# Value product of a decode attention block: weights stationary in four column groups instead of values stationary

## The chip, the cores and the metric

The kernel runs on one core of a Trainium2 chip. The metric is the device time of one execution in microseconds, as the median of several runs. They agree within 0.6% (kernel before), so differences under one per cent are read from ratios with an interval. A ratio is the mean time of one kernel's fast runs over the mean of the other's in the same rounds. It is therefore not quite the ratio of the medians that are quoted beside it.

## The reference, cut to what matters

The program is one decode step: four sequences, one new token each, 16 query heads in pairs over 8 key/value heads, a cache of 8192 positions and head size 256. A small MLP (cut here) gates the result.

```python
B, Sq, D = 4, 1, 448
Hq, Hkv, Sk, Dh = 16, 8, 8192, 256
q = (x @ wq)                                                  # x is layer-normalized
scores = einsum("bhqd,bhkd->bhqk", q, k) * Dh ** -0.5         # k, v repeated for 2 query heads
p = softmax(scores)
o = einsum("bhqk,bhkd->bhqd", p, v)                           # the value product
s = o.reshape(B, Sq, Hq * Dh) @ wo
out = x_in + s * silu(mlp(x))                                 # mlp cut
```

There are 4 x 8 = 32 pairs of sequence and key/value head. The text calls each of them a *head*. Each has 4 MB of K and 4 MB of V (bf16), which are read once: 268 MB of the 279 MB that the kernel loads.

## The kernel before

Per head, TensorE transposes K (128 transposes of 128x128), ScalarE and VectorE copy the transposes from PSUM, TensorE forms the scores (128 matmuls with the transposed K as stationary weights), and the value product of the head two places earlier is made with V as stationary weights. K and V have two buffers each. A new load is issued when TensorE has used up the buffer.

```python
def f_pv(h, lo, hi):                       # PE: value product of head h
    if lo == 0:
        take(pe, "v_ot"); take(pe, "dv%d" % (h % 2), 16)      # V has landed
    for i in range(lo, hi):                # 128 in all: two halves of Dh, 64 chunks of 128 positions
        dh, kk = divmod(i, NCH)
        ins = pe.matmul(psv[:, dh * PVW:(dh + 1) * PVW],      # out 128 x 32
                        vb[:, h % 2, kk, dh:DH:NHALF],        # stationary: V, 128 x 128
                        pT[:, h % 2, kk * REP:kk * REP + PVW],  # streaming: weights, 32 wide, 2 of use
                        start=(kk == 0), stop=(kk == NCH - 1))

def body(h):                               # PE, one head; the loop has two of them in one pass
    for j in range(NGR):                   # 16 groups of 8 transposes
        f_t(h, j)
        if j >= LAG: f_s(h, j - LAG)       # 8 score matmuls
        if j == J_SUM: f_sum(h - 1)
    tail = [the last three f_s] + [f_rmaxT(h), f_bc(h)]
    for i, f in enumerate(tail):
        f_pv(h - 2, PV_PARTS[i], PV_PARTS[i + 1]); f()

# SP queue: who releases a load
load_k(h): wait_ge(S["v_k"], h - 1)        # K of head h-2 transposed and copied
load_v(h): wait_ge(S["v_v"], h + 1)        # value product that last used the buffer is done
# ... (cut: projections, MLP, softmax pieces, the tail)
```

After the loop comes a *tail*: the value product of the last head but one, the output projection, and the last V, which arrives in four pieces.

Of the kernel before, what the change touches and what calls it, by code (L numbers as in the profile page):

```python
# [32 lines left out]
def bass_recurrent_scan__gqa_block_cached__mixer_s_mlp__decode_kernel(  # L33
# [40 lines left out]
    LAG = 3  # L74
    assert NGR == 16 and NGR % NST == 0 and NGR % RING == 0
    D_GROUPS = (0, 2, 4, 6, 8, 10, 12, 14, 15)
    NPV = NCH * NHALF
    PV_PARTS = (0, 12, 24, 44, 86, NPV)
    J_SUM = 3
    PVW = 32  # L80
    PIECES = (0, 32, 48, 56, NCH)
    NPIECE = len(PIECES) - 1
# [4 lines left out]
    with ExitStack() as es:  # L87
        def sb(name, shape, dty):
# [15 lines left out]
        xn2T = sb("xn2T", [P, DK, NHF, Bn], BF16)  # L104
        par = sb("par", [P, NHF], F32)
        hT = sb("hT", [P, NFK, NHF, Bn], BF16)
        rmax = sb("rmax", [P, REP], F32)
        negb = sb("negb", [P, 2, REP], F32)
        rowsum = sb("rowsum", [P, 2, REP], F32)
# [26 lines left out]
        S = {n: es.enter_context(nc.semaphore(n)) for n in (  # L136
            ["dx", "dwq", "dw3", "dw4", "dwo", "dk0", "dk1", "dv0", "dv1", "dout"]
            + ["dvl%d" % i for i in range(NPIECE)]
            + ["p_td", "p_ta", "p_sc", "p_m1", "p_m2", "p_m3", "p_pv", "p_x", "p_q", "p_h", "p_h2", "p_o"]
            + ["v_ev", "a_ev", "v_rmax", "v_diag", "v_neg", "v_ot", "a_exp", "g_q", "g_c",  # L140
               "v_s", "v_k", "v_v", "g_o", "g_p", "g_f", "v_xT", "v_qT", "v_hT", "v_bout", "v_c", "v_w", "a_c", "v_out"])}


        vflat = [vb[:, i].rearrange("p c d -> p (c d)") for i in range(2)]
# [73 lines left out]
        def prog_pool(gp):  # L218
            def put(h):
                b, g = divmod(h, HKV)  # L220
                gp.tensor_copy(OT[:, g, :, :, b],
                               otmp[:, h % 2].rearrange("p dh r -> p r dh")
                               ).then_inc(S["g_p"], 1)
                gp.wait_ge(S["g_p"], h + 1)
                gp.sem_inc(S["g_o"], 1)

            c = _Chain(gp, S["g_c"])
            c(gp.memset(ident_f[:, :], 0.0))
            c(gp.memset(ident_b[:, :], 0.0))
            c(gp.memset(ones_f[:, :], 1.0))  # L230
            c(gp.memset(pT[:, :, :].rearrange("p s n -> p (s n)"), 0.0))
            c(gp.memset(vflat[1][:, DK * HDH:NCH * DH], 0.0))
            c(gp.memset(vflat[0][:, DK * FH + NF * D:NCH * DH], 0.0))
            c(gp.memset(rowsum[:, :, :].rearrange("p s r -> p (s r)"), 1.0))
            c(gp.memset(rz[:, :, :].rearrange("p s r -> p (s r)"), 1.0))
            c.sync()
            for t in (ident_b, ident_f):
                c(gp.affine_select(out=t[:, :], in_=t[:, :], compare_op=ALU.not_equal, fill=1.0,  # L238
                                   base=0, pattern=[[-1, P]], channel_multiplier=1))
            gp.wait_ge(S["v_qT"], 1)  # L240
            for h in range(NH):
                b, g = divmod(h, HKV)
                if h >= 2:
                    gp.wait_ge(S["v_v"], h - 1)
                gp.tensor_copy(qc[:, h % 2], qT[:, b, g]).then_inc(S["g_q"], 1)  # L245
                if h >= 4:
                    put(h - 4)
            for h in range(NH, NH + 2):
                gp.wait_ge(S["v_v"], h - 1)
                put(h - 4)  # L250
            gp.wait_ge(S["g_p"], NH - 2)
            gp.sem_inc(S["g_f"], 1)

        def evac(engine, h, j):
# [8 lines left out]
        def prog_act(act):  # L263
            act.dma_start(x_sb[:, :], x2d).then_inc(S["dx"], 16)
            c = _Chain(act, S["a_c"])
            for k, col in ((1, 0), (2, 8)):
                act.wait_ge(S["v_w"], k)
                c(act.activation(st[:, col + 2:col + 3], st[:, col + 1:col + 2], ACT.Sqrt))
            act.wait_ge(S["v_w"], 3)
            c(act.activation(gel_b[:, :], gel_a[:, :], ACT.Tanh))  # L270
            act.wait_ge(S["v_w"], 4)
            c(act.activation(sg[:, :], bout[:, :], ACT.Tanh, scale=0.5))

            def exps(h):
                s = h % 2
                take(act, "v_neg")
                sc = psc[s][:, 0:NCH * REP].rearrange("p (k h) -> p k h", h=REP)
                pv_p = pT[:, s, 0:NCH * REP].rearrange("p (k h) -> p k h", h=REP)
                for hh in range(REP):
                    ins = act.activation(pv_p[:, :, hh], sc[:, :, hh], ACT.Exp,  # L280
                                         bias=negb[:, s, hh:hh + 1], scale=SCALE,
                                         accum_out=rowsum[:, s, hh:hh + 1])
                    if hh == REP - 1:
                        ins.then_inc(S["a_exp"], 1)

            with nc.Fori(0, NH // 2, engines=[mybir.EngineType.Activation]):
                for h in range(2):
                    for j in range(NGR):
                        if j not in D_GROUPS:
                            evac(act, h, j)  # L290
                    exps(h)
            act.wait_ge(S["v_out"], 1)
            store(act, 2)
            store(act, 3)

        def prog_dve(v):
# [31 lines left out]



            v.sem_inc(S["v_ot"], 1)
            v.sem_inc(S["g_o"], 4)
            v.sem_inc(S["a_exp"], 1)
            v.sem_inc(S["dv0"], 16)
            v.sem_inc(S["dv1"], 16)
            c(v.memset(h2_ps[:, 0:DQ], 0.0))
# [6 lines left out]
            xn_mark = c.n  # L343
            layernorm(xn_f, xn2_f, xn2_b, 8, 2)
            xn2_mark = c.n
            v.wait_ge(S["g_c"], 10)
            idv = ident_f[:, :].rearrange("p (m t) -> p t m", t=NHF)
            c(v.tensor_reduce(par[:, :], idv, AX.X, ALU.add))
            c.sync()
            for k, dst in ((0, xnT), (1, xn2T)):  # L350
                v.wait_ge(S["p_x"], k + 1)
# [62 lines left out]
                             ).then_inc(S["v_s"], 1)  # L414
                take(v, "v_s")

            def f_ot(h):
                take(v, "p_pv")
                take(v, "g_o")
                v.tensor_tensor(otmp[:, h % 2],  # L420
                                psv[:, 0:NHALF * PVW].rearrange("p (a n) -> p a n", a=NHALF)[
                                    :, :, 0:REP],
                                rz[:, h % 2, :].unsqueeze(1).broadcast_to([P, NHALF, REP]),
                                ALU.mult).then_inc(S["v_s"], 1)
                take(v, "v_s")
                v.sem_inc(S["v_ot"], 1)
                v.sem_inc(S["v_v"], 1)  # L427

            with nc.Fori(0, NH // 2, engines=[mybir.EngineType.DVE]):
                for h in range(2):  # L430
                    for j in range(NGR):
                        if j in D_GROUPS:
                            evac(v, h, j)
                        if j == J_SUM + 1:
                            f_rz(h - 1)
                    v.sem_inc(S["v_k"], 1)
                    f_rmax(h)
                    f_diag(h)
                    f_ot(h - 2)
                    f_negb(h)  # L440
            f_rz(NH - 1)
            for h in (NH - 2, NH - 1):
                b, g = divmod(h, HKV)
                take(v, "p_pv")
                for dh in range(NHALF):
                    src = psc[0] if (h == NH - 1 and dh == 1) else psv
                    ins = v.tensor_tensor(OT[:, g, :, dh, b],
                                          src[:, dh * PVW:dh * PVW + REP],
                                          rz[:, h % 2, :], ALU.mult)
                ins.then_inc(S["v_ot"], 1)  # L450
            v.wait_ge(S["p_o"], 1)
            c(v.tensor_tensor(res[:, :], o_ps[:, 0:DQ], sg[:, :], ALU.mult))  # L452
            c.sync()
# [1 line left out]
            return xn_mark, xn2_mark  # L455

        def prog_pe(pe, xn_mark, xn2_mark):
            pe.wait_ge(S["g_c"], 10)
            for k, (src, mark) in enumerate(((xn_b, xn_mark), (xn2_b, xn2_mark))):
                pe.wait_ge(S["v_c"], mark)  # L460
                for j in range(DK):
# [74 lines left out]
            def f_pv(h, lo, hi):  # L536
                if lo == 0:
                    take(pe, "v_ot")
                    take(pe, "dv%d" % (h % 2), 16)
                for i in range(lo, hi):  # L540
                    dh, kk = divmod(i, NCH)
                    ins = pe.matmul(psv[:, dh * PVW:(dh + 1) * PVW],  # L542
                                    vb[:, h % 2, kk, dh:DH:NHALF],
                                    pT[:, h % 2, kk * REP:kk * REP + PVW], start=(kk == 0), stop=(kk == NCH - 1))
                if hi == NPV:
                    ins.then_inc(S["p_pv"], 1)

            def body(h):
                for j in range(NGR):
                    f_t(h, j)  # L550
                    if j >= LAG:
                        f_s(h, j - LAG)
                    if j == J_SUM:
                        f_sum(h - 1)
                tail = [lambda j=j: f_s(h, j) for j in range(NGR - LAG, NGR)]
                tail += [lambda: f_rmaxT(h), lambda: f_bc(h)]
                for i, f in enumerate(tail):
                    f_pv(h - 2, PV_PARTS[i], PV_PARTS[i + 1])
                    f()
# [9 lines left out]
            def f_o(g):  # L569
# [6 lines left out]
                                        start=(k == 0), stop=(k == NKC - 1))  # L576
                return ins

            f_sum(h)
            pe.wait_ge(S["g_f"], 1)  # L580
            for g in range(HKV - 2):
                f_o(g)
            f_pv(h - 1, 0, NPV)
            take(pe, "v_ot")
            f_o(HKV - 2)
            for i in range(NPIECE):
                take(pe, "dvl%d" % i, 16)
                for dh in range(NHALF):
                    for kk in range(PIECES[i], PIECES[i + 1]):
                        ins = pe.matmul((psv, psc[0])[dh][:, dh * PVW:(dh + 1) * PVW],  # L590
                                        kn[:, 1 - h % 2, kk, dh:DH:NHALF],
                                        pT[:, h % 2, kk * REP:kk * REP + PVW], start=(kk == 0),
                                        stop=(kk == NCH - 1))
# [54 lines left out]
```

## Time and profile before

| | before |
|---|---|
| time, median of 4 runs | 664.05 us (662.49 to 665.04) |
| span of the profiled run | 660.5 us |
| loads | 279 MB, queue busy 98.8% of the span |
| TensorE busy | 81% |
| load rate between 334 and 640 us | 432 GB/s |

The first lines are from the page of the kernel before: the busy time of the engines, the DMA packets, the load queue's share, the groups of the transposes and the value product (line, engine, operation, operands, count, busy us, mean ns, idle time just before them and what ended it), and the K loads (count, size, median us from issue to landing).

```profile
PE 535.4 (81%) x13065; PEld 530.5 (80%) x13065; DVE 252.3 (38%) x548; ACT 254.9 (39%) x358; POOL 17.0 (3%) x76
...
DMA packets 12325, 279.20 MB, mean 423 GB/s; under 512 B 1172, under 2 KB 3224, under 8 KB 3736
...
q1 hardware_dynamic: 12288, 278.99, 98.8%
...
L504 PE MATMUL pst<-ident_b,kn 128*128 128x128 bf16 x4096 | 347.0, 241 | 92.7 <-PEq L216 92.6
...
L542 PE MATMUL psv<-pT,vb 128*128 128x32 bf16 x4224 | 130.3, 177 | 7.8 <-issue 7.7
L542 PEld LDWEIGHTS psv<-pT,vb 128*128 128x128 bf16 x4224 | 119.2, 97 | 8.8 <-issue 8.2
...
kn<-in_A_k_cache_dram SPq DMA_DIRECT2D x32, 4096.0 KB, 26.6
```

TensorE is busy for 81% of the span and the load queue for 98.8%. The waits view of the same kernel, between 330 and 640 us, tells what ended TensorE's idle time (total us, times, longest):

```profile
PE pst L504 <- PEq L216: 50.5, 16, 3.8
```

These 16 waits of 3.2 us on average are all before the first transposes of a head, that is, for its K. The windows view of 334 to 640 us has the load rate in its last column, the share of the DMA engines and TensorE's granted clock before it:

```profile
334.00:640.00 306.00, 258.25 (x6170) 256.75 (x6169) 117.06 (x236) 125.25 (x172) 4.59 (x29) 0.85 1.00 432
```

The timeline of the kernel before around the end of one head (start us, us, engine, what; in brackets the idle time before):

```profile
307.05 0.33 SPq L180 DMA_DIRECT2D kn<-in_A_k_cache_dram  x1
...
308.57 1.21 PE L542 MATMUL psv<-pT,vb 128*128 128x32 bf16 x42
...
309.63 0.27 PE L524 MATMUL psm<-ident_f,rmax 128*2 128x128 f32 x1
...
309.74 1.21 PE L542 MATMUL psv<-pT,vb 128*128 128x32 bf16 x42
...
311.64 0.33 SPq L188 DMA_DIRECT2D vb<-in_A_v_cache_dram  x1
...
314.40 3.57 PE L504 MATMUL pst<-ident_b,kn 128*128 128x128 bf16 x32 [3.15 <-PEq L216]
```

Here 42 value matmuls take 1.21 us. After the value product TensorE idles 3.15 us for the next K, which was asked for long before. A K load lands 26.6 us after its issue by the page's DMA part, though 4 MB take only 9.7 us at this rate. So loads queue up behind each other, and between 334 and 640 us the queue never runs dry (DMA share 1.00).

### The profile page before, as it was taken

Reading aid. Unit: us, or ns where it says so; the run is one execution under the profiler, and the core shown is the slowest. Engines: PE = TensorE matmul, PEld = TensorE weight load, DVE = VectorE, ACT = ScalarE, POOL = GpSimd, SP = SyncE. Lnnn points to the kernel's source line nnn. Section 1 sums busy time; section 2 is a strip of 40 time slices with the busy share of each in tenths; the row PEclk is TensorE's granted clock in tenths of the full one; section 3 lists DMA queues with packets and bytes.
Section 4 is the critical chain, followed back from the end, with each engine's and each line's share of the span. In section 5 each row is a group of like instructions: output and inputs, shape, how many; then the busy total and the mean of one; then the engine's idle time right before and its main releaser. Section 6 shows DMA issues by size and latency. Waiting matters only on the chain. (4 is left out here: it accounts for less than half of the span.)

```text
span 660.5 us, 29043 instructions
## 1 busy us (share of the span) xinstructions
PE 535.4 (81%) x13065; PEld 530.5 (80%) x13065; DVE 252.3 (38%) x548; ACT 254.9 (39%) x358; POOL 17.0 (3%) x76
## 2 busy tenths in 40 slices
PE   1487799967789878878987887898878898887886
PEld 1487799967789878878987787898878898887785
DVE  6233255433334433334443333433333343333340
ACT  1044355433344443334443343444333444433340
POOL 4000000000000000000000000000000000000000
PEclk9997799977898877889887788987878997787896
DMA  8999999999999999999999999999999999999995
GB/s 363 440 402 434 415 419 427 439 417 433 425 443 429 429 437 423 443 429 429 437 423 441 429 431 435 425 441 429 431 435 425 441 429 431 435 425 441 429 424 208
DMA packets 12325, 279.20 MB, mean 423 GB/s; under 512 B 1172, under 2 KB 3224, under 8 KB 3736
## 3 DMA queue, kind: packets, MB, share of 16 engines
q1 hardware_dynamic: 12288, 278.99, 98.8%
q8 instruction: 11, 0.18, 0.1%
q14 instruction: 2, 0.02, 0.0%
q10 hardware_dynamic: 24, 0.01, 0.0%
HBM read 278.99 MB, written 0.00 MB: 422 GB/s over the span
## 5 line engine op out<-in xcount | busy, mean ns | idle before, releaser
L504 PE MATMUL pst<-ident_b,kn 128*128 128x128 bf16 x4096 | 347.0, 241 | 92.7 <-PEq L216 92.6
L504 PEld LDWEIGHTS pst<-ident_b,kn 128*128 128x128 bf16 x4096 | 285.5, 110 | 94.6 <-issue 94.5
L259 DVE COPY kT<-pst 128x1024 bf16<-128x1024 bf16 x288 | 197.8, 692 | 269.4 <-DVEq L216 269.3
L261 ACT ACTIVATE kT<-pst 128x1024 bf16<-128x1024 bf16 x224 | 229.1, 1024 | 184.2 <-ACTq L216 184.2
L516 PE MATMUL psc<-qc,kT 128*128 128x2 bf16 x4096 | 176.3, 164 | 3.3 <-issue 3.3
L516 PEld LDWEIGHTS psc<-qc,kT 128*128 128x128 bf16 x4096 | 156.4, 97 | 3.4 <-issue 3.4
L542 PE MATMUL psv<-pT,vb 128*128 128x32 bf16 x4224 | 130.3, 177 | 7.8 <-issue 7.7
L542 PEld LDWEIGHTS psv<-pT,vb 128*128 128x128 bf16 x4224 | 119.2, 97 | 8.8 <-issue 8.2
L280 ACT ACTIVATE pT<-psc,negb 128x64 bf16<-128x64 f32 x64 | 20.2, 329 | 183.8 <-ACTq L216 183.8
L396 DVE TENSOR_REDUCE rmax<-psc 128x2 f32<-128x128 f32 x32 | 9.3, 292 | 42.0 <-DVEq L216 42.0
L245 POOL COPY qc<-qT 128x4 bf16<-128x4 bf16 x32 | 5.9, 188 | 585.5 <-DVEq L427 575.7
L401 DVE TENSOR_REDUCE gmax<-psm 2x1 f32<-2x128 f32 x32 | 8.9, 279 | 29.0 <-DVEq L216 29.0
L533 PE MATMUL psm<-rowsum,ones_f 128*128 128x2 f32 x66 | 15.5, 304 | 1.7 <-PEq L216 1.7
L533 PEld LDWEIGHTS psm<-rowsum,ones_f 128*128 128x128 f32 x66 | 13.4, 253 | 1.7 <-issue 1.7
L420 DVE TENSOR_TENSOR otmp<-psv,rz 128x4 bf16<-128x4 f32 x32 | 5.2, 163 | 22.9 <-DVEq L216 22.9
L280 ACT ACTIVATION_READ_ACCUMULATOR pT<-psc,negb 128x1 f32 x64 | 12.5, 196 | 0.0
L528 PE MATMUL psm<-diag,ones_f 2*128 2x2 f32 x64 | 12.5, 263 | 0.0
L462 PE MATMUL pst<-ident_b,xn_b 4*128 4x4 bf16 x14 | 0.6, 161 | 13.5 <-DVE xn_b L327 8.8
L462 PEld LDWEIGHTS pst<-ident_b,xn_b 4*128 4x128 bf16 x14 | 0.5, 100 | 13.5 <-POOL ident_f L238 8.8
L528 PEld LDWEIGHTS psm<-diag,ones_f 2*128 2x128 f32 x64 | 9.8, 190 | 1.0
L409 DVE COPY negb<-psm 128x2 f32<-128x2 f32 x32 | 5.1, 159 | 14.1 <-DVEq L216 14.1
L524 PE MATMUL psm<-ident_f,rmax 128*2 128x128 f32 x32 | 8.8, 276 | 0.0
(72 smaller groups left out, 79.1 us busy)
## 6 DMA issues: line engine op xcount, KB each, us to landing
kn<-in_A_k_cache_dram SPq DMA_DIRECT2D x32, 4096.0 KB, 26.6
vb<-in_A_v_cache_dram SPq DMA_DIRECT2D x31, 4096.0 KB, 31.6
vb<-in_A_wq_dram SPq DMA_DIRECT2D x1, 3584.0 KB, 11.2
wo_sb<-in_A_wo_dram SPq DMA_DIRECT2D x1, 3584.0 KB, 46.9
vb<-in_B_w_dram SPq DMA_DIRECT2D x2, 1568.0 KB, 16.9
kn<-in_A_v_cache_dram SPq DMA_DIRECT2D x1, 2048.0 KB, 26.7
kn<-in_A_v_cache_dram SPq DMA_DIRECT2D x1, 1024.0 KB, 29.3
kn<-in_A_v_cache_dram SPq DMA_DIRECT2D x2, 512.0 KB, 30.4
```

Source lines behind the costliest of these rows:

```text
L245: gp.tensor_copy(qc[:, h % 2], qT[:, b, g]).then_inc(S["g_q"], 1)
L259: engine.tensor_copy(dst, src).then_inc(S["v_ev"], 1)
L261: engine.activation(dst, src, ACT.Copy).then_inc(S["a_ev"], 1)
L280: ins = act.activation(pv_p[:, :, hh], sc[:, :, hh], ACT.Exp, bias=negb[:, s, hh:hh + 1], scale=SCALE, accum_out=rowsum[:, s, hh:hh + 1])
L396: v.tensor_reduce(rmax[:, :], psc[h % 2][:, 0:NCH * REP].rearrange("p (k h) -> p h k", h=REP), AX.X, ALU.max).then_inc(S["v_rmax"], 1)
L401: v.tensor_reduce(gmax[:, :], psm[0:REP, 0:P], AX.X, ALU.max).then_inc(S["v_s"], 1)
L504: ins = pe.transpose(dst[:, t * P:(t + 1) * P], kn[:, h % 2, GC * j + kl, half * P:(half + 1) * P], ident_b[:, :])
L516: ins = pe.matmul(psc[h % 2][:, kk * REP:(kk + 1) * REP], kT[:, j % RING, t * P:(t + 1) * P], qc[:, h % 2, half, :], start=(half == 0), st ...
L524: pe.transpose(psm[0:REP, 0:P], rmax[:, :], ident_f[:, :]).then_inc(S["p_m1"], 1)
L528: pe.matmul(psm[:, P:P + REP], ones_f[0:REP, :], diag[:, :], start=True, stop=True).then_inc(S["p_m2"], 1)
L533: pe.matmul(psm[:, P + REP:P + 2 * REP], ones_f[:, :], rowsum[:, h % 2, :], start=True, stop=True).then_inc(S["p_m3"], 1)
L542: ins = pe.matmul(psv[:, dh * PVW:(dh + 1) * PVW], vb[:, h % 2, kk, dh:DH:NHALF], pT[:, h % 2, kk * REP:kk * REP + PVW], start=(kk == 0), ...
```

## The change

The intent is to make the value product shorter on TensorE. The weights (two columns per chunk) become the stationary operand and V streams 256 wide, so a head needs 64 matmuls instead of 128, with weight loads of 128x2 instead of 128x128. Four chunks at a time write to four groups of output partitions, 32 apart (the *column groups*). That matmuls in different groups overlap was an assumption of the author's; experiment 3 measured it (27 ns per matmul in four groups, 109 ns in one). The result comes out as 2 rows x 256 in each of the four groups of partitions. VectorE copies it to SBUF, and two fp32 products with a 0/1 matrix `sel` sum the four groups and turn the result back to 128 x 2. To get these steps off the end of a head, the broadcast of the maximum, the exponentials and the sum move into the next head's transposes.

```diff
-    NPV = NCH * NHALF
-    PV_PARTS = (0, 12, 24, 44, 86, NPV)
-    J_SUM = 3
+    NCG = 4
+    CGW = P // NCG
+    PV_PARTS = (0, 8, 16, 28, NCH)
+    J_BC, J_TR, J_SUM = 1, 3, 8
@@ PE
-                for i in range(lo, hi):
-                    dh, kk = divmod(i, NCH)
-                    ins = pe.matmul(psv[:, dh * PVW:(dh + 1) * PVW],
-                                    vb[:, h % 2, kk, dh:DH:NHALF],
-                                    pT[:, h % 2, kk * REP:kk * REP + PVW], start=(kk == 0), stop=(kk == NCH - 1))
+                for kk in range(lo, hi):
+                    o = kk % NCG * CGW
+                    ins = pe.matmul(psv[o:o + REP, 0:DH],
+                                    pT[:, h % 2, kk * REP:(kk + 1) * REP], vb[:, h % 2, kk, :],
+                                    start=(kk < NCG), stop=(kk >= NCH - NCG))
+            def f_tr(h):
+                take(pe, "v_po")
+                for dh in range(NHALF):
+                    o = DH + dh * REP
+                    ins = pe.matmul(psv[:, o:o + REP], po[:, dh:DH:NHALF], sel[:, :],
+                                    start=True, stop=True)
+                ins.then_inc(S["p_tr"], 1)
             def body(h):
                 for j in range(NGR):
                     f_t(h, j)
                     if j >= LAG:
                         f_s(h, j - LAG)
+                    if j == J_BC:
+                        f_bc(h - 1)
+                    if j == J_TR:
+                        f_tr(h - 3)
                     if j == J_SUM:
                         f_sum(h - 1)
@@ DVE
+            def f_po(h):
+                take(v, "p_pv")
+                v.sem_inc(S["v_v"], 1)
+                v.tensor_copy(po[:, :], psv[:, 0:DH]).then_inc(S["v_po"], 1)
@@ ACT
-                    exps(h)
+                        if j == J_BC + 2:
+                            exps(h - 1)
... (cut: semaphores, the order of the tail, last V pieces into two other PSUM banks, setup of sel)
```

More of the change, by code (lines that the diff above doesn't have):

```diff
@@ L106, in bass_recurrent_scan__gqa_block_cached__mixer_s_mlp__decode_kernel @@
         hT = sb("hT", [P, NFK, NHF, Bn], BF16)
+        sel = sb("sel", [P, REP], F32)
+        po = sb("po", [P, DH], F32)
         rmax = sb("rmax", [P, REP], F32)
@@ L138, in bass_recurrent_scan__gqa_block_cached__mixer_s_mlp__decode_kernel @@
             + ["dvl%d" % i for i in range(NPIECE)]
-            + ["p_td", "p_ta", "p_sc", "p_m1", "p_m2", "p_m3", "p_pv", "p_x", "p_q", "p_h", "p_h2", "p_o"]
+            + ["p_td", "p_ta", "p_sc", "p_m1", "p_m2", "p_m3", "p_tr", "p_pv", "p_x", "p_q", "p_h", "p_h2", "p_o"]
             + ["v_ev", "a_ev", "v_rmax", "v_diag", "v_neg", "v_ot", "a_exp", "g_q", "g_c",
-               "v_s", "v_k", "v_v", "g_o", "g_p", "g_f", "v_xT", "v_qT", "v_hT", "v_bout", "v_c", "v_w", "a_c", "v_out"])}
+               "v_s", "v_k", "v_v", "v_po", "v_o", "g_o", "g_p", "g_f", "v_xT", "v_qT", "v_hT", "v_bout", "v_c", "v_w", "a_c", "v_out"])}
         vflat = [vb[:, i].rearrange("p c d -> p (c d)") for i in range(2)]
@@ L220, in put @@
                 b, g = divmod(h, HKV)
+                gp.wait_ge(S["v_o"], h + 4)
                 gp.tensor_copy(OT[:, g, :, :, b],
@@ L233, in prog_pool @@
             c(gp.memset(vflat[0][:, DK * FH + NF * D:NCH * DH], 0.0))
-            c(gp.memset(rowsum[:, :, :].rearrange("p s r -> p (s r)"), 1.0))
+            c(gp.memset(diag[:, :], 0.0))
+            c(gp.memset(po[:, :], 0.0))
             c(gp.memset(rz[:, :, :].rearrange("p s r -> p (s r)"), 1.0))
@@ L245, in prog_pool @@
                 gp.tensor_copy(qc[:, h % 2], qT[:, b, g]).then_inc(S["g_q"], 1)
-                if h >= 4:
-                    put(h - 4)
-            for h in range(NH, NH + 2):
-                gp.wait_ge(S["v_v"], h - 1)
-                put(h - 4)
-            gp.wait_ge(S["g_p"], NH - 2)
+                if h >= 5:
+                    put(h - 5)
+            for h in range(NH - 5, NH - 3):
+                put(h)
+            gp.wait_ge(S["g_p"], NH - 3)
             gp.sem_inc(S["g_f"], 1)
@@ L290, in prog_act @@
                             evac(act, h, j)
-                    exps(h)
+                        if j == J_BC + 2:
+                            exps(h - 1)
+            exps(NH - 1)
             act.wait_ge(S["v_out"], 1)
@@ L327, in layernorm @@
                     c(v.tensor_copy(dst_b[:, (1 - t) * (DK - 1), :, t], sv[:, nj]))
-            v.sem_inc(S["v_ot"], 1)
-            v.sem_inc(S["g_o"], 4)
-            v.sem_inc(S["a_exp"], 1)
+            c(v.memset(psc[1][:, 0:NCH * REP], 0.0))
+            c(v.memset(psv[:, 0:DH], 0.0))
+            c.sync()
+            v.sem_inc(S["v_diag"], 1)
+            v.sem_inc(S["v_po"], 1)
+            v.sem_inc(S["g_o"], 5)
             v.sem_inc(S["dv0"], 16)
@@ L345, in prog_dve @@
             xn2_mark = c.n
-            v.wait_ge(S["g_c"], 10)
+            v.wait_ge(S["g_c"], 11)
             idv = ident_f[:, :].rearrange("p (m t) -> p t m", t=NHF)
             c(v.tensor_reduce(par[:, :], idv, AX.X, ALU.add))
+            c(v.tensor_reduce(sel[:, :], ident_f[:, :].rearrange(
+                "p (j r) -> p r j", j=NCG)[:, 0:REP], AX.X, ALU.add))
             c.sync()
@@ L415, in f_rz, with f_ot @@
                 take(v, "v_s")
-            def f_ot(h):
+            def f_po(h):
                 take(v, "p_pv")
-                take(v, "g_o")
-                v.tensor_tensor(otmp[:, h % 2],
-                                psv[:, 0:NHALF * PVW].rearrange("p (a n) -> p a n", a=NHALF)[
-                                    :, :, 0:REP],
+                v.sem_inc(S["v_v"], 1)
+                v.tensor_copy(po[:, :], psv[:, 0:DH]).then_inc(S["v_po"], 1)
+            ot_src = psv[:, DH:DH + NHALF * REP].rearrange("p (a r) -> p a r", a=NHALF)
+            def f_ot(h, last=False):
+                b, g = divmod(h, HKV)
+                take(v, "p_tr")
+                if not last:
+                    take(v, "g_o")
+                dst = OT[:, g, :, :, b].rearrange("p r a -> p a r") if last else otmp[:, h % 2]
+                v.tensor_tensor(dst, ot_src,
                                 rz[:, h % 2, :].unsqueeze(1).broadcast_to([P, NHALF, REP]),
@@ L426, in f_ot @@
                 v.sem_inc(S["v_ot"], 1)
-                v.sem_inc(S["v_v"], 1)
+                v.sem_inc(S["v_o"], 1)
             with nc.Fori(0, NH // 2, engines=[mybir.EngineType.DVE]):
@@ L433, in prog_dve @@
                             evac(v, h, j)
-                        if j == J_SUM + 1:
+                        if j == J_BC + 1:
+                            f_negb(h - 1)
+                        if j == J_TR + 1:
+                            f_ot(h - 3)
+                        if j == J_SUM + 2:
                             f_rz(h - 1)
@@ L438, in prog_dve @@
                     f_diag(h)
-                    f_ot(h - 2)
-                    f_negb(h)
-            f_rz(NH - 1)
-            for h in (NH - 2, NH - 1):
-                b, g = divmod(h, HKV)
-                take(v, "p_pv")
-                for dh in range(NHALF):
-                    src = psc[0] if (h == NH - 1 and dh == 1) else psv
-                    ins = v.tensor_tensor(OT[:, g, :, dh, b],
-                                          src[:, dh * PVW:dh * PVW + REP],
-                                          rz[:, h % 2, :], ALU.mult)
-                ins.then_inc(S["v_ot"], 1)
+                    f_po(h - 2)
+            h = NH - 1
+            f_negb(h)
+            f_ot(h - 2, True)
+            f_rz(h)
+            f_po(h - 1)
+            f_ot(h - 1, True)
+            b, g = divmod(h, HKV)
+            take(v, "p_pv")
+            for dh in range(NHALF):
+                ins = v.tensor_tensor(OT[:, g, :, dh, b], pst[1 + dh][:, 0:REP],
+                                      rz[:, h % 2, :], ALU.mult)
+            ins.then_inc(S["v_ot"], 1)
             v.wait_ge(S["p_o"], 1)
@@ L457, in prog_pe @@
         def prog_pe(pe, xn_mark, xn2_mark):
-            pe.wait_ge(S["g_c"], 10)
+            pe.wait_ge(S["g_c"], 11)
             for k, (src, mark) in enumerate(((xn_b, xn_mark), (xn2_b, xn2_mark))):
@@ L539, in f_pv @@
                     take(pe, "dv%d" % (h % 2), 16)
-                for i in range(lo, hi):
-                    dh, kk = divmod(i, NCH)
-                    ins = pe.matmul(psv[:, dh * PVW:(dh + 1) * PVW],
-                                    vb[:, h % 2, kk, dh:DH:NHALF],
-                                    pT[:, h % 2, kk * REP:kk * REP + PVW], start=(kk == 0), stop=(kk == NCH - 1))
-                if hi == NPV:
-                    ins.then_inc(S["p_pv"], 1)
+                for kk in range(lo, hi):
[3 more added lines that the diff above has]
+                                    start=(kk < NCG), stop=(kk >= NCH - NCG))
+                if hi == NCH:
+                    ins.then_inc(S["p_pv"], 1)
+            def f_tr(h):
+                take(pe, "v_po")
+                for dh in range(NHALF):
+                    o = DH + dh * REP
+                    ins = pe.matmul(psv[:, o:o + REP], po[:, dh:DH:NHALF], sel[:, :],
+                                    start=True, stop=True)
+                ins.then_inc(S["p_tr"], 1)
             def body(h):
@@ L555, in body @@
                 tail = [lambda j=j: f_s(h, j) for j in range(NGR - LAG, NGR)]
-                tail += [lambda: f_rmaxT(h), lambda: f_bc(h)]
+                tail += [lambda: f_rmaxT(h)]
                 for i, f in enumerate(tail):
@@ L577, in f_o @@
                 return ins
+            f_bc(h)
+            f_tr(h - 2)
+            pe.wait_ge(S["g_f"], 1)
+            for g in range(HKV - 3):
+                f_o(g)
             f_sum(h)
-            pe.wait_ge(S["g_f"], 1)
-            for g in range(HKV - 2):
-                f_o(g)
-            f_pv(h - 1, 0, NPV)
+            f_pv(h - 1, 0, NCH)
+            f_o(HKV - 3)
+            f_tr(h - 1)
             take(pe, "v_ot")
@@ L589, in prog_pe @@
                     for kk in range(PIECES[i], PIECES[i + 1]):
-                        ins = pe.matmul((psv, psc[0])[dh][:, dh * PVW:(dh + 1) * PVW],
+                        ins = pe.matmul(pst[1 + dh][:, 0:PVW],
                                         kn[:, 1 - h % 2, kk, dh:DH:NHALF],
```

## The prediction

> **What bounds the kernel now.** The loads do. The page's DMA line gives 279 MB, and the load queue is busy for 98.8% of 16 engines' span. Between 334 and 640 us the windows view shows a flat 432 GB/s[...]. In the timeline two loads of 4 MB are issued per head, 19.8 us apart; a K load lands 26.7 us after its issue (the page's DMA part), so others are always queued ahead of it. TensorE looks busy (81%), but in the waits view it idles 50 us between 330 and 640 us, in 16 waits of some 3.2 us, each before a head's first transposes, for its K. Its clock drops in such a wait: 32 transposes then take 3.3 to 3.6 us[...]. So TensorE has 3 to 4 us of slack per head, and a shorter value product only lengthens the wait.
>
> **What the change removes.** Per head, 128 matmuls of N=32 with 128x128 weights. In the timeline 42 of them take 1.21 us: 29 ns each, 3.7 us per head.
>
> **What it adds.** 64 matmuls with two-column weights and N=256 in four column groups; two fp32 products of N=2 (about 0.7 us, an estimate from today's, 0.35 us); on VectorE a 128x256 fp32 copy (0.3 to 0.5 us, an estimate from the 0.29 us reduction of 128x128). A 128-wide transpose takes 76 ns, so N=256 should take 110 to 150 ns. If four groups overlap[...], 64 cost 1.8 to 3 us; if not, 7 to 9 us (estimates). TensorE's work per head changes by -1.5 to +5 us, of which 3 to 4 us are covered by the wait for K and the returning clock. Most likely it falls by about 1 us and the wait grows by as much.
>
> **What it moves.** Broadcast, exponentials and sum go into the next head's transposes. ScalarE is busy 1.02 us of every 1.29 us there, so 1.05 us of exponentials stalls the transposes a little, within slack.
>
> **On the critical path** lie only the two ends. Start: until 90 us the rate dips (344 to 418 GB/s in several 4 us windows), while TensorE waits 2.5 to 3.6 us inside the first loop pass for instructions; the loop becomes a sixth shorter, so one such fetch goes: 0 to 2 us. End: the last data land at about 654.5 us (packet records), the span ends at 660.5 us. The value product of the last head but one (3.3 us, plus 1.7 us of instruction wait) precedes the last pieces; if it shrinks, up to 1.4 us are gained, less the new turn and copy (about 1 us).
>
> **Prediction:** 662 us, range 655 to 668. Chances: faster by over 2% 0.03, within 2% 0.94, slower by over 2% 0.03.
>
> **What would show it.** Load rate again 431 to 433 GB/s in the middle, heads 19.8 us apart, K waits of 4 to 5 us, TensorE busy share below 78%, value product 2 to 2.5 us per head. A gain, if any, before 90 us or after 650 us.
>
> **What would make it wrong.** Column groups that run one after the other[...], so that a head takes over 20.3 us of TensorE time: heads spread, loads starve, and it gets slower by 2 to 5%.[...]

The terms at the two ends are 0 to 2 us at the start and 1.4 - 1 = 0.4 us at the end, which from 664.05 us gives 661.7 to 664 us. Per head the terms give 1.8 + 0.7 - 3.7 = -1.2 us to 3 + 0.7 - 3.7 = 0 us if the groups overlap, and 4.0 to 6.0 us if not, beside the -1.5 to +5 us. The 1.8 us are a quarter of 64 x 110 ns; the 3 us, which leave room for an incomplete overlap, are the author's guess, and that the groups overlap at all was not shown by then. The clock is read from the windows view of the kernel before: 1.00 between 308.57 and 311.00 us, and 0.50 between 314.40 and 318.00 us, after a wait of 3.15 us. Between 330 and 640 us its clock records show 16 such stretches at 0.50, of 3.4 or 6.8 us each, beside the 16 waits. The 76 ns of a transpose are a group of eight in 0.61 us; from start to start in a group of 32 it is 56 ns (experiment 3).

## The result, and the profile after

The changed kernel takes 660.52 us (median of 4 runs, 660.21 to 660.95) against 664.05 us. The ratio is 0.9949, with a 95% interval of 0.9927 to 0.9972. A later session gave 660.44 us against 662.44 us and a ratio of 0.9969 (0.9952 to 0.9986). The gain is real and small: some 2 to 3.5 us, far below the 2% at which the record would call a kernel faster.

The same lines of the page after:

```profile
PE 531.3 (81%) x11091; PEld 481.5 (73%) x11091; DVE 260.7 (40%) x585; ACT 252.6 (38%) x362; POOL 17.0 (3%) x76
...
DMA packets 12324, 279.18 MB, mean 424 GB/s; under 512 B 1172, under 2 KB 3224, under 8 KB 3736
...
q1 hardware_dynamic: 12288, 278.99, 98.9%
...
L528 PE MATMUL pst<-ident_b,kn 128*128 128x128 bf16 x4096 | 345.5, 238 | 101.2 <-PEq L219 99.7
...
L566 PE MATMUL psv<-vb,pT 128*2 128x256 bf16 x2112 | 84.8, 284 | 2.5 <-issue 1.8
L566 PEld LDWEIGHTS psv<-vb,pT 128*2 128x2 bf16 x2112 | 39.8, 84 | 10.9 <-issue 2.8
...
L576 PE MATMUL psv<-sel,po 128*128 128x2 f32 x136 | 25.1, 289 | 0.7 <-PEq L219 0.6
```

The value product's busy time fell from 130.3 to 84.8 us and its weight loads from 119.2 to 39.8 us, a third. New are the turning products (25.1 us; the timeline shows four matmuls per head for the two in the code). The load queue is at 98.9%. TensorE's busy share is still 81%. (The page adds up the modelled durations of single matmuls, 284 ns for one of these, joined where they overlap; so the share is no measure of what a head costs.)

The waits for K and the windows of the same stretches, after:

```profile
PE pst L528 <- PEq L219: 57.5, 16, 5.2
```

```profile
334.00:640.00 306.00, 252.73 (x5270) 230.57 (x5274) 121.13 (x257) 124.78 (x180) 4.77 (x30) 0.88 1.00 432
```

The load rate in the middle is the same 432 GB/s. The waits for K grew from 50.5 to 57.5 us: what TensorE saved became waiting. (7.0 us in 16 heads are 0.44 us per head, more than the 0.25 us that experiment 5 finds; the granted clock was 0.88 instead of 0.85, so the two figures are not of the same clock.) The end of a head in the timeline after:

```profile
307.01 0.33 SPq L183 DMA_DIRECT2D kn<-in_A_k_cache_dram  x1
...
308.11 0.50 PE L566 MATMUL psv<-vb,pT 128*2 128x256 bf16 x12
...
308.82 1.15 PE L566 MATMUL psv<-vb,pT 128*2 128x256 bf16 x36
...
309.90 0.27 PE L548 MATMUL psm<-ident_f,rmax 128*2 128x128 f32 x1
...
310.93 0.33 SPq L191 DMA_DIRECT2D vb<-in_A_v_cache_dram  x1
...
310.99 0.42 DVE L431 COPY po<-psv 128x256 f32<-128x256 f32 x1
...
312.62 1.05 PE L528 MATMUL pst<-ident_b,kn 128*128 128x128 bf16 x16 [2.45 <-PEq L219]
```

From 12 to 36 matmuls the time grows from 0.50 to 1.15 us, so one matmul of 256 columns costs (1.15 - 0.50) / 24 = 27 ns.

So where do the 1.8 us between the two profiled spans (660.5 and 658.7) come from? The records of the load packets can be summed up to show how far the stream of loads lags behind a stream that starts at 2 us and runs at 432 GB/s throughout. This is worked out from the records, not a view of the profile:

```
lag of the loads (us) at     40 us   65 us   90 us   150 us   300 us   600 us   last landing   span
before                        1.2     3.0     4.3      4.9      4.5      4.8      654.6        660.5
after                         1.3     2.9     3.4      3.4      3.4      3.6      653.7        658.7
```

The stream of loads loses over 1 us less before 150 us, and from there both run at the same rate; at the last landing 0.9 us of it are left. The other 0.9 us lie after the last landing: 5.9 us before, 5.0 us after. Nothing was gained in the 500 us between. A second profiled run of the changed kernel (after_again) has the same figures: a lag of 3.6 us at 600 us, the last landing at 653.5 us and 5.0 us from there to the end. Of the kernel before there is this one profiled run. Between the medians of all runs lie 2.0 us (second session) and 3.5 us (first), as the profiled run of before was one of its faster ones; how the rest is spread over the two ends is not known.

### The profile page after: what moved, and what is told of

Read it like the earlier page. It is cut to its first block, busy times and chain, and to the rows that moved or that the text cites. A ratio compares the mean times of both kernels' runs of the same rounds, so it can differ in the third digit from the quotient of the medians.

```text
span 658.7 us, 25245 instructions
## 1 busy us (share of the span) xinstructions
PE 531.3 (81%) x11091; PEld 481.5 (73%) x11091; DVE 260.7 (40%) x585; ACT 252.6 (38%) x362; POOL 17.0 (3%) x76
## 3 DMA queue, kind: packets, MB, share of 16 engines
q1 hardware_dynamic: 12288, 278.99, 98.9%
## 5 line engine op out<-in xcount | busy, mean ns | idle before, releaser
L528 PEld LDWEIGHTS pst<-ident_b,kn 128*128 128x128 bf16 x4096 | 277.6, 108 | 106.4 <-issue 105.8
L566 PE MATMUL psv<-vb,pT 128*2 128x256 bf16 x2112 | 84.8, 284 | 2.5 <-issue 1.8
L566 PEld LDWEIGHTS psv<-vb,pT 128*2 128x2 bf16 x2112 | 39.8, 84 | 10.9 <-issue 2.8
L576 PE MATMUL psv<-sel,po 128*128 128x2 f32 x136 | 25.1, 289 | 0.7 <-PEq L219 0.6
L576 PEld LDWEIGHTS psv<-sel,po 128*128 128x128 f32 x136 | 23.0, 237 | 0.9 <-issue 0.9
L552 PEld LDWEIGHTS psm<-diag,ones_f 2*128 2x128 f32 x66 | 12.7, 239 | 6.0 <-issue 4.6
L552 PE MATMUL psm<-diag,ones_f 2*128 2x2 f32 x66 | 15.4, 301 | 1.1 <-PEq L219 0.9
L431 DVE COPY po<-psv 128x256 f32<-128x256 f32 x33 | 14.0, 425 | 4.8 <-DVEq L219 4.1
L557 PE MATMUL psm<-rowsum,ones_f 128*128 128x2 f32 x66 | 12.4, 257 | 0.0
L557 PEld LDWEIGHTS psm<-rowsum,ones_f 128*128 128x128 f32 x66 | 10.3, 196 | 0.2 <-issue 0.2
```

What stands on the lines that cost most here:

```text
L431: v.tensor_copy(po[:, :], psv[:, 0:DH]).then_inc(S["v_po"], 1)
L528: ins = pe.transpose(dst[:, t * P:(t + 1) * P], kn[:, h % 2, GC * j + kl, half * P:(half + 1) * P], ident_b[:, :])
L552: pe.matmul(psm[:, P:P + REP], ones_f[0:REP, :], diag[:, :], start=True, stop=True).then_inc(S["p_m2"], 1)
L557: pe.matmul(psm[:, P + REP:P + 2 * REP], ones_f[:, :], rowsum[:, h % 2, :], start=True, stop=True).then_inc(S["p_m3"], 1)
L566: ins = pe.matmul(psv[o:o + REP, 0:DH], pT[:, h % 2, kk * REP:(kk + 1) * REP], vb[:, h % 2, kk, :], start=(kk < NCG), stop=(kk >= NCH - NCG))
L576: ins = pe.matmul(psv[:, o:o + REP], po[:, dh:DH:NHALF], sel[:, :], start=True, stop=True)
```

## The experiments

Theory A, that of the prediction: the loads bind. In the loop TensorE has slack, so the value product could take less or somewhat more time without effect; only the two ends count. Rival B: TensorE binds (it is the busiest engine), and the change gave back what it gained. Rival C: the gain lies in one end only.

Some of the kernels below compute a wrong result. The comparison with the reference passed for all of them, also for those. It therefore does not see the attention term, and says little about this part.

### 1. Only 4 of 64 value matmuls in the loop

```diff
-                for kk in range(lo, hi):
+                some = lo == 0 and hi == NCH           # the tail keeps all
+                for kk in range(lo, hi if some else min(hi, NCG)):
```

> The changed kernel with only 4 of the 64 value matmuls in the loop (wrong result on purpose; the tail keeps its own). Theory (the loads bind): TensorE loses about 1.6 us per head, the wait for K before the transposes grows by as much (57 us in 16 waits becomes about 80 us between 330 and 640 us), and the time stays within 0.4% of the changed kernel: 658 to 662 us. Rival (TensorE, 81% busy, binds): 32 x 1.6 = 51 us less, about 610 us.

Measured: 661.40 us, ratio to the kernel before 0.9987 (0.9956 to 1.0018). Rival B, which wanted 610 us, is out. The wait for K did not grow to 80 us, though:

```profile
PE pst L528 <- PEq L219: 55.2, 16, 6.4
```

```profile
334.00:640.00 306.00, 243.02 (x4290) 232.53 (x4288) 120.33 (x252) 124.04 (x176) 4.77 (x30) 0.77 1.00 432
```

The time that the matmuls left went into a lower granted clock (0.77 after 0.88), at which the other matmuls take longer (in pv_x2 eight transposes took 1.01 us at a clock of 0.50 and 0.61 us at 1.00), and into the steps around the maximum that are no longer covered (9.4 us in 16 waits for the maximum's transpose). That part of the expectation was wrong; the total was right.

### 2. The same from the kernel before: 2 of 128 in the loop

```diff
+                cut = (lo > 0 or hi < NPV) == CUT_LOOP
                 for i in range(lo, hi):
                     dh, kk = divmod(i, NCH)
+                    if cut and kk > 0:
+                        continue
```

> The kernel before with only 2 of the 128 value matmuls of each head in the loop (wrong result on purpose; the tail keeps its 128). This frees 3.6 us of TensorE per head, ten times the 0.36 us that the change frees. Theory (the loads bind): at most the loads' short start is gained, 0 to 2 us: ratio to before 0.996 to 1.000, about 661 to 664 us, and the K wait grows from 3.2 to about 7 us per head. Rival (the value product costs time in the loop): 32 x 3.6 = 115 us less.

Measured: 661.88 us, ratio 0.9989 (0.9972 to 1.0007), in five rounds. Taking out all but 2 of the 128 value matmuls of each head in the loop gains at most 0.3%. The lag of the loads at 150 us was 3.1 us instead of 4.9, a gain of the same kind as in the changed kernel, but 6.6 us passed from the last landing to the end. The waits for K were 61.6 us in 16, not 7 us each; again the clock was lower (0.78 over the whole run, 0.86 before).

### 3. One column group, and two

```diff
-                    o = kk % NCG * CGW
+                    o = 0                      # one_group; two_groups: kk % 2 * CGW
```
(with `start` and `stop` set for the first and last matmul of each group)

> The changed kernel with all 64 value matmuls in one column group (right result). If the four groups overlap, one matmul now follows the other every 107 to 115 ns instead of every 27 ns, and a head takes about 5.2 us more of TensorE: 14.1 + 5.2 = 19.3 us, just under the 19.43 us that two 4 MB loads take. Theory (the loads bind, the wait is slack): 660 to 680 us, so at most 3% slower for a value product four times as long. Rival (TensorE binds): 32 x 5.2 = 166 us more. If the groups do not overlap, nothing changes: 660 us and 27 ns.

> The changed kernel with two column groups instead of four (right result): one matmul follows the other every 54 ns, the value product of a head takes about 1.75 us more, TensorE 15.9 us per head. Theory (slack): 660 to 663 us, the K waits between 330 and 640 us fall from 57 us to about 30 us. Rival (TensorE binds): 56 us more.

The lines of the 36 matmuls from the timelines of one_group and two_groups, in that order:

```profile
242.12 1.47 PE L566 MATMUL psv<-vb,pT 128*2 128x256 bf16 x12
...
243.80 4.09 PE L566 MATMUL psv<-vb,pT 128*2 128x256 bf16 x36
```

```profile
306.26 0.82 PE L566 MATMUL psv<-vb,pT 128*2 128x256 bf16 x12
...
307.30 2.13 PE L566 MATMUL psv<-vb,pT 128*2 128x256 bf16 x36
```

By the same subtraction a matmul costs (4.09 - 1.47) / 24 = 109 ns in one group, (2.13 - 0.82) / 24 = 55 ns in two and 27 ns in four. The groups overlap fully: 109 / 27 = 4.0. The 109 ns are also what 256 columns take without any overlap, as an estimate from the transposes: 32 of them, 128 columns each, take 1.80 us (experiment 5), so 56 ns each and 112 ns for twice the width. All of these are read as the cost of one more matmul in a long stream.

The times: two_groups 662.30 us (ratio 0.9989, 0.9960 to 1.0018). TensorE spends 1.7 us more per head (5.00 instead of 3.28 us from the score group before the product to the transpose of the maximum) and the time stays within the interval; the waits for K between 330 and 640 us fell to 32.0 us, as forecast:

```profile
PE pst L528 <- PEq L219: 32.0, 15, 3.5
```

one_group took 682.40 us, 3.1% more than before, a little above the range forecast. A head of it takes 19.33 us of TensorE (K loads issued at 239.73 and 259.06 us), just under the 19.43 us that its two loads take, and TensorE is busy all the time:

```profile
92.00:150.00 58.00, 57.86 (x990) 50.17 (x988) 22.61 (x48) 23.26 (x33) 0.81 (x5) 1.00 1.01 433
334.00:640.00 306.00, 305.25 (x5189) 264.24 (x5187) 119.00 (x253) 121.72 (x174) 5.07 (x32) 1.00 0.99 425
```

The loads kept 433 GB/s to begin with, and the lag was 4.5 us at 600 us, no more than in the kernel before (4.8 us). The 17.1 us between its span (675.8) and that of the changed kernel come at the end. At 14.1 us per head TensorE catches up with the loads in the first heads and then waits for them; at 19.33 us it never does, and ends its last head some 16 us later. The last head's maximum is transposed at 653.83 us instead of 637.40, the last V lands 3.6 us later (657.3), and 18.5 us instead of 5.0 us pass from there to the end. So a value product four times as long does not slow the loads in the loop; what it costs shows at the end.

### 4. The product repeated

```diff
+                again = list(range(NCH)) * (REPEAT - 1) if hi == NCH and lo > 0 else []
-                for kk in range(lo, hi):
+                for kk in list(range(lo, hi)) + again:
```

> The changed kernel with the value product of each head of the loop done three times (right result, the last pass counts): about 3.5 us more TensorE per head, 17.6 us, still under 19.43 us. Theory: the wait for K falls to about 1.8 us per head (mean), time 659 to 666 us. Rival (TensorE binds): 32 x 3.5 = 112 us more, about 772 us.

> The same five times: 7.0 us more, about 21.1 us per head, now above the 19.43 us of the loads. Theory: TensorE binds here, no wait for K after the first heads, heads 21.1 us apart, time 31 + 32 x 21.1 + 10 to 20 = 715 to 730 us, and the load rate in the middle falls to about 397 GB/s. If there is another limit than these two, the time falls outside 705 to 740 us.

Measured: 904.67 us (three times) and 1052.24 us (five times). Both expectations failed by far. The DMA queues of pv_x3, from its page, point to the cause (packets, MB, share of the engines):

```profile
q1 hardware_dynamic: 12288, 278.99, 76.4%
q8 instruction: 147, 2.41, 1.2%
```

The queue named "instruction" moved 147 packets of 16 KB where the changed kernel has 10 (pv_x5: 179). In the waits view TensorE's value matmuls waited 73.0 us in 30 waits for nothing that the profile shows:

```profile
PE psv L568 <- issue: 73.0, 30, 3.6
```

The loop of pv_x3 has 914 matmuls in a pass, each with its weight load. 147 packets in 16 passes are about 9 per pass (the packet records show nine in a pass), of 2.41 MB / 147 = 16.4 KB each: instructions are fetched anew in each pass, where the changed kernel has 10 packets in all. That TensorE waits for such packets is seen in the kernel before: it stood still for 1.5 to 3.6 us four times in the first pass, and each time resumed 1.2 to 1.4 us after a packet had ended. In pv_x3 the timeline between 430 and 490 us, a little over one pass, has four waits of this kind, of 0.95 to 3.52 us. Why they come again was not shown; at which length of the loop they begin to is known only from pv_x2, below. These two runs do not test theory A. The next one was made to repair that:

> The changed kernel with the value product of each head of the loop done twice: TensorE 15.9 us per head as in two_groups, but with as many matmuls in one pass of the loop as the kernel before (about 786 against 778), where pv_x3 had 914. Theory (pv_x3 was slow[...]: 147 instruction packets of 16 KB against 10[...]): 660 to 664 us with 10 to 12 instruction packets. Rival (repeating the product on the same PSUM bank is slow of itself, about 7 us per repeat): about 780 us.

Measured: 667.25 us, ratio 1.0060 (1.0028 to 1.0093), with 11 instruction packets. The cliff is gone: with 786 matmuls in a pass the packets do not come again, with 914 they do (147). The rival (780 us) is out. It is still 3 us above the range. The windows view of the start of pv_x2 shows where the time went (the last columns are the granted clock, the share of the DMA engines and GB/s):

```profile
66.00:70.00 4.00, 4.00 (x57) 4.00 (x56) 1.46 (x3) 1.42 (x2) 0.00 (x0) 0.50 0.34 143
70.00:74.00 4.00, 4.00 (x78) 3.76 (x75) 1.86 (x3) 1.65 (x2) 0.00 (x0) 0.67 0.01 4
74.00:78.00 4.00, 4.00 (x141) 3.13 (x137) 0.46 (x2) 0.00 (x0) 0.00 (x0) 1.00 1.04 369
```

The loads stood still here. TensorE's line in the timeline before that:

```profile
64.62 0.35 PE L541 MATMUL psc<-qc,kT 128*128 128x2 bf16 x8 [4.42 <-issue]
```

In the first pass of the loop TensorE waited 4.42 us, and resumed 1.3 us after an instruction packet had ended (62.37 to 63.29 us by the packet records). The next K load was then issued at 73.55 us instead of 64.95 us, when the queue was already empty. The wait alone does not make these 8.6 us. The head began 3.5 us later, after a longer product and another such wait of 2.70 us. This wait was 2.9 us longer than its like in the changed kernel (1.48 us). And after it the granted clock was 0.50, at which a group of transposes and scores took 1.07 us instead of 0.65 us until 72.5 us. The lag of the loads grew from 3.2 to 11.0 us between 65 and 80 us and stayed at that to the end. So the early stretch does count: what was lost there was not won back, as the loads were no faster later (432 GB/s between 250 and 400 us).

### 5. The loads made shorter

```diff
-                    sp.dma_start(vflat[h % 2], src.rearrange("p c d -> p (c d)")
+                    sp.dma_start(vflat[h % 2][:, 0:NCH // 4 * DH],
+                                 src[:, 0:NCH // 4, :].rearrange("p c d -> p (c d)")
```

> The kernel before with only a quarter of V loaded for all heads but the last (wrong result on purpose; the value product still reads the whole tile, part of it stale). A head's loads then take about 12.1 us, less than TensorE's 14.49 us per head at full clock (read between 90 and 105 us, where no K was waited for). Theory: TensorE now binds, heads 14.5 us apart, no K waits, about 518 to 526 us.

> The changed kernel with the same cut of the loads. TensorE takes 14.13 us per head at full clock. Theory (the change frees only 0.36 us of TensorE per head net, and this shows once the loads don't bind): heads 14.1 us apart, about 500 to 508 us, that is 2.5 to 3.5% below quarter_v_before. Rival (the new value product frees 2 us per head, as its own instructions suggest, and only the loads hid it): 32 x 2 = 64 us, 12%, below.

Measured: 519.41 us and 512.69 us; ratios to the unchanged kernel before of the same rounds 0.7843 and 0.7725, so the change gains 1 - 0.7725 / 0.7843 = 1.5% here. The first time lies in the range expected, the second above it (500 to 508 us). TensorE binds now: there is no wait of TensorE in the waits view between 100 and 480 us in either kernel, and it is busy throughout.

```profile
250.00:400.00 150.00, 149.47 (x4094) 148.67 (x4092) 76.41 (x156) 78.64 (x113) 3.13 (x20) 1.00 0.89 362
```

```profile
250.00:400.00 150.00, 149.49 (x3491) 135.88 (x3489) 80.02 (x170) 81.11 (x114) 3.45 (x22) 1.00 0.91 370
```

Two heads take 28.77 us before (K loads issued at 209.90 and 238.67 us) and 28.27 us after (210.13 and 238.40). Per head that is 0.25 us, or 8 us in 32 heads, and 6.7 us were measured. I had expected 2.5 to 3.5%: the 0.36 us came from one head, but the two heads of a pass differ (14.30 and 14.46 us before), so it was too large. The rival of 2 us per head is out.

The same two traces show where TensorE's saving went. Each figure is a distance between starts in the timeline of one head (for the product, less 0.20 us for each of the four groups of score matmuls within it):

```
TensorE, us per head              before    after
value product, with its borders    3.30      2.48     (64 x 27 ns = 1.73, the rest at 8 borders with other matmuls)
first 32 transposes                1.80      2.00     (now in two parts, around the broadcast)
turning product                     -        0.48
```

So 0.82 us are saved and 0.68 us given back, before anything is hidden by the loads. A border costs about (2.48 - 1.73) / 8 = 0.09 us after the change, against (3.30 - 128 x 0.025) / 10 = 0.01 us before; for what reason was not shown. The table is of the shorter of the two heads of a pass. In the other one the kernel before takes 0.17 us more from the broadcast to the first transposes, and the changed kernel does not, which makes up most of the rest to 0.25 us.

### 6. The tail

> The kernel before with the loop untouched and only 2 of the 128 value matmuls of the last head but one in the tail (wrong result on purpose). Theory (part of the change's gain lies in the tail, where this product precedes the last pieces[...]): 0.5 to 1.5 us less than before, the time from the last landing to the end falls from 5.9 us to about 5.0 us. Rival (the tail is set by the last landing alone): no difference.

Measured: 661.98 us, ratio 0.9989 (0.9969 to 1.0009), so no difference that is clear of zero. Its loads lagged more than before in the profiled run (5.8 us at 150 us), but the point is the end, which took 6.2 us from the last landing (654.04 us) instead of the 5.0 us expected. The last pieces in the timelines of b_tail_2, of the kernel before and of the changed kernel:

```profile
655.53 0.24 PE L594 MATMUL psv<-pT,kn 128*128 128x32 bf16 x2 [1.84 <-issue]
```

```profile
655.83 0.40 PE L590 MATMUL psc<-pT,kn 128*128 128x32 bf16 x8 [0.52 <-issue]
```

```profile
654.29 0.59 PE L630 MATMUL pst<-pT,kn 128*128 128x32 bf16 x16 [0.62 <-PEq L219]
```

In the first two the engine waits in the middle of a piece that has already landed ("issue": nothing that the profile shows), after an instruction packet that came at 652.96 and 653.47 us by the records. In the changed kernel the wait (0.62 us) is before the last piece, for its data. The product of the tail itself, in the kernel before and in the changed kernel:

```profile
646.08 3.31 PE L542 MATMUL psv<-pT,vb 128*128 128x32 bf16 x122
...
651.01 0.35 PE L542 MATMUL psv<-pT,vb 128*128 128x32 bf16 x6 [1.61 <-issue]
```

```profile
642.90 3.52 PE L566 MATMUL psv<-vb,pT 128*2 128x256 bf16 x64 [0.65 <-PEq L219]
```

In this run of the changed kernel the product was not shorter, as the granted clock was 0.53 over its 3.52 us (3.52 x 0.53 = 1.87 us at 1.00, as an estimate); in after_again it took 1.92 us, and the end was 5.0 us after the last landing in both. So a shorter product is not what shortened the tail. What differs is that TensorE waits for each of the last pieces in the changed kernel, while in the kernel before it is late and waits for none of them. A product that is long enough to make TensorE late does cost: in two_groups it took 4.95 us, TensorE then went through the last V without a wait (653.16 to 656.54 us), and 7.0 us passed from the last landing (653.19 us) to the end. That TensorE was late in the kernel before because of the waits for instructions (1.61 and 0.52 us) is inferred from the packets beside them; no run took these waits away by themselves.

### 7. K loads in two halves

```diff
+                for i in range(2):
+                    if h >= 2:
+                        sp.wait_ge(S["v_k"], 2 * (h - 1) - 1 + i)
+                    lo, hi = i * NCH // 2, (i + 1) * NCH // 2
+                    sp.dma_start(kn[:, h % 2, lo:hi, :]..., src[:, lo:hi, :]...)
... (VectorE gives v_k after groups 8 and 15)
```

> The changed kernel with each K load in two halves, the first issued when half of the head before last has been transposed (right result). Theory (in the first five heads a load is issued only 2.8 to 5 us before the queue ahead of it empties, and packets then take 0.2 to 0.9 us longer): the 1 to 2 us lost between 45 and 90 us come back, 0.5 to 1.5 us faster than the changed kernel, 659 to 660 us. Rival (the dips come from elsewhere): no difference to the changed kernel. It can't gain more, as the loads are at 432 GB/s for the rest.

> The changed kernel as it is, beside the others on the same chip: 660 to 662 us, ratio to before 0.994 to 0.998; from the last landing to the end about 5.0 us.

Measured on one chip: split_k 663.07 us, the changed kernel 660.44 us (ratio to before 0.9969), so the halves are 0.4% slower. The lag at 90 us was 3.2 us against 3.4 in both runs of the changed kernel: there was nothing left to win. Later it grew steadily, from 3.5 us at 150 us to 6.0 at 640 us, where the changed kernel stays at 3.4 to 3.6. The packet records show the size of it: a packet of a half (16 KB) took 0.615 us and one of a whole load (32 KB) 1.217 us, so a byte took 1.0% longer. For half of the bytes of 490 us that is 2.4 us, and the lag grew by 2.5 us. Why two small packets take longer than a large one is open. The changed kernel was thus the fastest correct kernel tried.

## Why the prediction was right

- **The loads bind: right.** 432 GB/s in the middle before and after, and with all but a sliver of the value product taken out of the loop the time moved by 0.1% (experiments 1 and 2). Only when the loads were cut did TensorE's saving show (experiment 5).
- **662 us, within 2%: right.** 660.52 us was measured, inside 655 to 668 us.
- **Four groups overlap: right.** 27, 55 and 109 ns per matmul for four, two and one group. The 2.48 us of the product lie in the range of 1.8 to 3 us.
- **The value product took 3.7 us: too large.** It takes 3.30 us. I divided 1.21 us by 42, which counts in what a group takes beyond the cost of one more matmul: 12 matmuls take 0.45 us, so one more costs (1.21 - 0.45) / 30 = 25 ns.
- **TensorE saves about 1 us per head, waits of 4 to 5 us, busy share below 78%: all too large.** The saving is 0.25 us, the waits grew from 3.2 to 3.6 us, and the busy share stayed at 81%. Mis-sized were the product before (by 0.4 us) and the borders: the parts into which the product and the transposes are cut cost 0.2 us in the transposes alone. The loads hid all of this, so the time could not show these errors.
- **Heads 19.8 us apart: slightly off.** That was the distance of two neighbours. On average it is 19.4 us, two loads of 9.7 us; after the change the distances alternate.
- **The start: right in size, and shown to count by pv_x2.** The instruction packets fell from 11 to 10 and the loads lag 1.2 us less. TensorE's waits of this kind in the first pass sum up to 9.3 us before, and to 4.0 and 6.1 us in the two profiled runs of the changed kernel; in b_tail_2, with the loop of the kernel before, they were 10.2 us and the lag 5.8 us. Which part the packet fewer has in this and which the shorter work is not separated; loop_4, with the least work, lagged 4.0 us at 150 us, so a short loop body alone does not secure the gain.
- **The end: wrong in its reason, and too small.** I laid it to a shorter product ahead of the last pieces: up to 1.4 us, less about 1 us for the new steps, so some 0.4 us. It was 0.9 us. b_tail_2 took that product out and gained nothing clear of zero, and in the profiled run of the changed kernel the product of the tail was no shorter than before. That a gain came at this end all the same is partly luck.
- **Rival C (one end only): not settled.** The profiled runs show a gain at both ends. b_loop_2 had the one at the start (last landing at 652.2 us) with a longer end (6.6 us), and in all gained nothing clear of zero. No run has the gain at one end with the other end as before.

## What to carry to other kernels

Before you shorten work on the busiest engine, see what ends its idle time: here every head ended in a wait for loads that ran at a flat rate, so ten times the saving gained nothing clear of the noise (experiment 2). What did count here was any moment in which the loads were asked for late, above all in the first pass of the loop (7.8 us of lag in pv_x2), and what follows the last landing (18.5 us in one_group, 5.0 us in the changed kernel). Count the instruction packets on the page when a loop's body grows: from 786 to 914 matmuls per pass, a sixth more, they went from 11 to 147 and the kernel became over a third slower (667 to 905 us).
